# First batch's weight pieces placed in each engine's order group by group, with three raw buffers of their own and late side loads

## Chip, cores, metric

One core of one Trainium2 chip. The metric is the device time of a run in microseconds. The kernel before has a median of 818.7 us in the runs at hand at the start.

## The reference, cut to what matters

```python
# x (8, 8, 512, 64), state (8, 8, 32, 64)  -> attention both ways, concatenated: 4352 tokens x 512
# then, with w_in (512, 2048) and w_out (2048, 512):
h = x @ w_in
sp = np.maximum(h, 0.0) + np.log1p(np.exp(-np.abs(h)))   # softplus
g = h * erf(sp)
return (g @ w_out).astype(np.float32)
```

The weights arrive as float64, 16 MB in all. The kernel makes float32 of them on the chip.

## The kernel before

Batch 0 is worked in four groups of 512 hidden features. Its weights come in 16 pieces of 1 MB (two of w_in and two of w_out for each group). A piece is fetched raw, then converted by two passes of ScalarE (ACT) and three of VectorE (DVE):

```python
def weight(dst, src, shape, tag, bufs):
    ...
    raw = act.tile([P, 2 * shape[0] * i], U32, name=tag, bufs=bufs)
    nc.sync.dma_start(out=raw.rearrange("p (o i) -> p o i", i=2 * i), in_=src.bitcast(U32))
    ...
    nc.scalar.activation(out=dst, in_=hi.bitcast(F32), func=ACTF.Copy, scale=2.0 ** -112)   # L108
    nc.scalar.activation(out=lo, in_=lo, func=ACTF.Copy, scale=2.0 ** -29)                  # L109
    nc.vector.tensor_scalar(d, d, 3, None, op0=ALU.logical_shift_left)                      # L110
    nc.vector.tensor_tensor(d, d, lo, op=ALU.add)                                           # L111
    nc.vector.scalar_tensor_tensor(out=d, in0=hi, ...)                                      # L112

def weights_in(j):   weight(w_in[:, j], ..., "raw", 2)
def weights_out(g):  weight(w_out[:, t:t + 2, :], ..., "hs", 2)    # two pieces
...
def hidden(b, fts, t0, n):
    hs = act.tile([P, 4, S], F32, name="hs")          # the same two "hs" buffers as w_out's raw pieces
    s = act.tile([P, 4, S], F32, name="s")
    for i in range(4):
        hp = ps_h.tile([P, S], F32, name="h")         # two banks
        ...                                           # matmuls, L269
        nc.scalar.activation(out=s[:, i, :], in_=hp, func=ACTF.Softplus)    # L271
        nc.vector.tensor_copy(hs[:, i, :], hp)                              # L272
    nc.scalar.activation(out=s, in_=s, func=ACTF.Erf)                       # L273
    return s, hs, nc.vector.tensor_tensor(s, s, hs, op=ALU.mult)            # L274
...
for g, (first, second) in enumerate(groups):
    if b == 0 and g > 0:
        weights_in(2 * g)
        weights_in(2 * g + 1)
        mixed(0, g)                # PE mixes states into w_in: m (L253), copies by ACT and DVE (L255)
        weights_out(g)
        if g == 2:
            load_st()              # states of batches 1 to 7
    ...
    before, gT = gT, first()       # hidden(g)
    ...
    if pending is not None:
        pending()                  # project(g - 1), L279
```

The program's text is not the order in the queues: a scheduler at build time puts each engine's instructions in order by what it expects to be ready first. `tc.issue_after(x)` says that what is traced inside comes behind x on x's engine. It is an order of issue, no wait.

Of the kernel before, what the change touches and what calls it, by code (L numbers as in the profile page):

```python
# [8 lines left out]
F32 = mybir.dt.float32  # L9
U32 = mybir.dt.uint32  # L10
ALU = mybir.AluOpType
ACTF = mybir.ActivationFunctionType
# [4 lines left out]
def kernel(  # L17
# [17 lines left out]
    nc = tc.nc  # L35
    B, H, S, D = x.shape
    Ns = state.shape[2]
    d_model, d_ff = moe_w_in.shape
    P = 128
    NI = H // 2  # L40
    NC = S // P
    NK = d_model // P
    NF = d_ff // P
    GF = 4
    NG = NF // GF
# [5 lines left out]
    const = ctx.enter_context(tc.tile_pool(name="const", bufs=1))  # L51
# [5 lines left out]
    act = ctx.enter_context(tc.tile_pool(name="act", bufs=2))  # L57
# [11 lines left out]
    def load_x(b, queues=(nc.sync,)):  # L69
        t = xin.tile([P, NC, H, D], F32, name="x")  # L70
        for h in range(H):
            queues[h % len(queues)].dma_start(out=t[:, :, h, :],
                                              in_=x[b, h].rearrange("(p c) d -> p c d", c=NC))
        x_t[b] = t
# [3 lines left out]
    for e in range(2):  # L78
        nc.sync.dma_start(out=st[:, 0, D * e:D * e + D],
                          in_=state[0].rearrange("(i e) n d -> e i n d", e=2)[e])  # L80
# [9 lines left out]
    w_in = const.tile([P, NF // 2, NK, 2 * P], F32, name="w_in")  # L90
    w_out = const.tile([P, NF, d_model], F32, name="w_out")

    def weight(dst, src, shape, tag, bufs):




        if src.dtype == F32:
            nc.sync.dma_start(out=dst, in_=src)
            return  # L100
        i = shape[1]
        raw = act.tile([P, 2 * shape[0] * i], U32, name=tag, bufs=bufs)
        nc.sync.dma_start(out=raw.rearrange("p (o i) -> p o i", i=2 * i), in_=src.bitcast(U32))
        words = raw.rearrange("p (n w) -> p n w", w=2)
        lo, hi = words[:, :, 0], words[:, :, 1]
        dst = dst.rearrange("p o i -> p (o i)")
        d = dst.bitcast(U32)
# [4 lines that stand above are left out]
        nc.vector.scalar_tensor_tensor(out=d, in0=hi, scalar=0x80000000, in1=d,  # L112
                                       op0=ALU.bitwise_and, op1=ALU.bitwise_or)
# [3 lines left out]
    def weights_in(j):  # L117
        weight(w_in[:, j],
               moe_w_in[:, 2 * P * j:2 * P * j + 2 * P].rearrange("(k p) f -> p k f", p=P),
               (NK, 2 * P), "raw", 2)  # L120

    def weights_out(g):
        for t in range(GF * g, GF * g + GF, 2):
            weight(w_out[:, t:t + 2, :],
                   moe_w_out[P * t:P * t + 2 * P].rearrange("(t p) e -> p t e", p=P),
                   (2, d_model), "hs", 2)

    spare = ps_o.tile([P, d_model], F32, name="o3")

# [10 lines left out]
    def states(b):  # L140

        ps = ps_at.tile([P, P], F32, name="at")
        nc.tensor.transpose(out=ps, in_=st[:, b, :], identity=ident)
        stT[b] = keep.tile([P, P], F32, name="stT")
        nc.scalar.copy(stT[b], ps)
# [92 lines left out]
    def mixed(b, g, parts=1):  # L238

        m_t[b, g] = mix.tile([P, 2, gw], F32, name="m")  # L240
        for j in range(parts):
            ends = mixed_part(b, g, j, parts)
        return ends

    def mixed_part(b, g, j, parts):
        n = gw // parts
        mg = m_t[b, g][:, :, n * j:n * j + n]
        fs = slice(2 * g + j, 2 * g + j + 2 // parts)
        ps = [ps_at.tile([P, gw], F32, name="at")[:, 0:n] for _ in range(2)]
        for i in range(NI):  # L250
            for e in range(2):
                r, q = slice(D * e, D * e + D), slice(Ns * i, Ns * i + Ns)
                nc.tensor.matmul(out=ps[e][q, :], lhsT=stT[b][r, q],  # L253
                                 rhs=w_in[r, fs, i, :], start=True, stop=True)
        return nc.scalar.copy(mg[:, 0], ps[0]), nc.vector.tensor_copy(mg[:, 1], ps[1])  # L255

    def hidden(b, fts, t0, n):



        hs = act.tile([P, 4, S], F32, name="hs")
        s = act.tile([P, 4, S], F32, name="s")
        m = S // n
        for i in range(4):
            hp = ps_h.tile([P, S], F32, name="h")
            for j in range(m):
                ops = pairs(b, fts[m * i + j], slice(t0, t0 + n))
                for k, (lhsT, rhs) in enumerate(ops):
                    nc.tensor.matmul(out=hp[:, n * j:n * j + n], lhsT=lhsT, rhs=rhs,  # L269
                                     start=(k == 0), stop=(k == len(ops) - 1))  # L270
            nc.scalar.activation(out=s[:, i, :], in_=hp, func=ACTF.Softplus)  # L271
            nc.vector.tensor_copy(hs[:, i, :], hp)  # L272
        nc.scalar.activation(out=s, in_=s, func=ACTF.Erf)  # L273
        return s, hs, nc.vector.tensor_tensor(s, s, hs, op=ALU.mult)  # L274

    def project(gT, g, acc):
        for r in range(NC):
# [12 lines left out]
    E2 = d_model // 2  # L290
# [4 lines left out]
    T = {}  # L295

    def combine_w():
        T[1], T[2] = (act.tile([P, 2 * GF * P * 2], U32, name="raw", bufs=2).bitcast(F32)
                      .rearrange("p (g i e) -> p g i e", i=GF, e=E2) for _ in range(2))
        T[4] = const.tile([P, NG // 2, GF, E2], F32, name="T4")  # L300
        sub = lambda o, x, y: nc.vector.tensor_tensor(o, x, y, op=ALU.subtract)  # L301
        sub(T[1], B12, B11)
        sub(T[2], B22, T[1])
        sub(T[4], B21, T[2])

        def last():
            sub(B12, B22, B12)
            T[3] = B12
        return last
# [42 lines left out]
    def put_x(b, h):  # L352
        rows = out[TB * b:TB * b + S].rearrange("(p c) e -> c p e", c=NC)

        def go(r, ot):
            nc.sync.dma_start(out=rows[2 * h + r], in_=ot)
        return go
# [7 lines left out]
    def pairs(b, f, toks):  # L365
        g, fs = f // GF, slice(P * (f % GF), P * (f % GF) + P)
        if b < B:
            return [(m_t[b, g][:, e, fs], aT[b][:, e, toks]) for e in range(2)]
        return [(w_in[:, f // 2, k, P * (f % 2):P * (f % 2) + P], sT[:, k].rearrange("p b n -> p (b n)")[:, toks])
                for k in range(NK)]  # L370
# [4 lines left out]
    def plain(b):  # L375

        box = []

        def project_(g, gT):
            if g == 0:  # L380
                box.extend(tiles(NC))
            project(gT, g, box)
            if g == NG - 1:
                store(box, lambda r, ot: put_x(b, r // 2)(r % 2, ot))
        for g in range(NG):
            yield lambda g=g: hidden(b, range(GF * g, GF * g + GF), 0, S), \
                lambda gT, g=g: project_(g, gT[0])
# [26 lines left out]
    rest, on_act, on_dve = attention(0, begin)  # L414
    with tc.issue_after(on_act.ins), tc.issue_after(on_dve.ins):
        weights_in(1)
    on_act, on_dve = mixed(0, 0, 2)
    with tc.issue_after(on_act.ins), tc.issue_after(on_dve.ins):
        weights_out(0)
    pending = last = gT = None  # L420
    for b in range(B + 1):
        if b == 0:
            groups = plain(b)
        elif b < B:
            groups = fast(b, 2, lambda h, b=b: put_x(b, h))
        else:
            groups = fast(b, 1, lambda h: put_s)
        for g, (first, second) in enumerate(groups):
            if b == 0 and g > 0:
                weights_in(2 * g)  # L430
                weights_in(2 * g + 1)
                mixed(0, g)
                weights_out(g)
                if g == 2:
                    load_st()
            if b + 1 < B and g == (2 if b == 0 else 0):
                load_x(b + 1)
                states(b + 1)
            before, gT = gT, first()
            if b == 0 and g == 2:  # L440
                with tc.issue_after(before[2].ins):
                    rest()
            if pending is not None:
                pending()
            if last is not None:
                last()
                last = None
            if b == 0 and g == NG - 1:
                last = combine_w()

            def pending(gT=gT, second=second):
                second(gT)
            if b + 1 < B and (b or g > 1):
                for i in [g] if b else [2 * g - 4, 2 * g - 3]:
                    mixed(b + 1, i)
                if g == (NG - 1 if b == 0 else 1):
                    attention(b + 1)[0]()
# [31 lines left out]
```

## Time and profile before

| | before |
|---|---|
| median of the runs at the start, us | 818.7 |
| span of the profiled run, us | 815.4 |
| first hidden matmul of batch 0, us | 25.05 |
| mix of group 1 starts (second w_in piece of group 1 done), us | 44.20 |
| TensorE's longest wait from 20 to 62 us | 6.4 us, for the copy L272 |
| granted clock, 25 to 60 us | 0.82 |

A matmul in float32 leaves two records. In a row, a record of 128x512 takes 0.43 to 0.45 us at the full granted clock (eight in 3.60 us) and up to twice that at half. In a timeline row the columns are start, duration, engine, line, operation, tiles, count, and in brackets the idle time just before it with what ended it.

### The profile page before, as it was taken

Reading aid. Unit: us, or ns where it says so; the run is one execution under the profiler, and the core shown is the slowest. Engines: PE = TensorE matmul, PEld = TensorE weight load, DVE = VectorE, ACT = ScalarE, POOL = GpSimd, SP = SyncE. Lnnn points to the kernel's source line nnn. Section 1 sums busy time; section 2 is a strip of 40 time slices with the busy share of each in tenths; the row PEclk is TensorE's granted clock in tenths of the full one; section 3 lists DMA queues with packets and bytes.
Section 4 is the critical chain, followed back from the end, with each engine's and each line's share of the span. In section 5 each row is a group of like instructions: output and inputs, shape, how many; then the busy total and the mean of one; then the engine's idle time right before and its main releaser. Section 6 shows DMA issues by size and latency. Waiting matters only on the chain.

```text
span 815.4 us, 10488 instructions
## 1 busy us (share of the span) xinstructions
PE 790.0 (97%) x4460; PEld 605.4 (74%) x4460; DVE 428.6 (53%) x626; ACT 369.4 (45%) x465; POOL 0.7 (0%) x6
## 2 busy tenths in 40 slices
PE   7679999999999999999999999999999999999997
PEld 5234334678888788878887888878887888888886
DVE  3899545438454644556453844555454745443431
ACT  5688534545333833345333633373334533333220
POOL 0000000000000000000000000000000000000000
PEclk9699999999999999999999999999999999999999
DMA  9774401201100020002000110000000000000000
GB/s 276 214 258 146 112 1 39 66 0 41 39 1 26 1 79 0 27 1 79 0 27 1 29 50 1 27 1 27 1 27 1 27 1 27 1 26 1 27 1 26
DMA packets 47414, 35.27 MB, mean 43 GB/s; under 512 B 36872, under 2 KB 36872, under 8 KB 47368
## 3 DMA queue, kind: packets, MB, share of 16 engines
q1 hardware_dynamic: 45256, 34.09, 13.6%
q10 hardware_dynamic: 2112, 0.52, 0.3%
q8 instruction: 35, 0.57, 0.3%
q14 instruction: 11, 0.09, 0.0%
HBM read 25.69 MB, written 8.91 MB: 42 GB/s over the span
## 4 chain that ended last, share of the span: by engine, by line
PE 83%; ACT 3%; DVE 3%; DMA 1%; issue 1%
PE o L332 45%; PE h L269 27%; PE at L253 3%; PE o L279 3%; PE at L154 1%; PE at L177 1%; ACT L271 1%; PE at L212 1%; PE at L224 1%; PE at L195 1%; ACT s L271 1%; DVE s L274 1%; DMA hs<-in_moe_w_out_dram 1%; DVE raw L301 1%; ACT s L273 0%
## 5 line engine op out<-in xcount | busy, mean ns | idle before, releaser
L269 PE MATMUL h<-aT,m 128*128 128x256 f32 (+1 forms) x960 | 245.3, 403 | 10.6 <-DVE hs L272 7.2
L269 PEld LDWEIGHTS h<-aT,m 128*128 128x128 f32 x960 | 179.1, 192 | 76.3 <-issue 36.7
L272 DVE COPY hs<-h 128x512 f32<-128x512 f32 x136 | 93.4, 689 | 200.9 <-ACT s L271 200.9
L271 ACT ACTIVATE s<-h 128x512 f32<-128x512 f32 x136 | 80.4, 597 | 172.1 <-PE h L269 171.7
L274 DVE TENSOR_TENSOR s<-s,hs 128x2048 f32<-128x2048 f32 x34 | 77.9, 2292 | 77.1 <-ACT s L273 77.1
L332 PE MATMUL o<-raw,hs 128*128 128x256 f32 x480 | 115.7, 380 | 0.0
L332 PE MATMUL o<-w_out,s 128*128 128x256 f32 x480 | 115.0, 379 | 0.6 <-DVE s L274 0.6
L332 PE MATMUL o<-w_out,hs 128*128 128x256 f32 x480 | 113.4, 379 | 0.0
L332 PEld LDWEIGHTS o<-w_out,hs 128*128 128x128 f32 x480 | 91.2, 190 | 12.4
L332 PEld LDWEIGHTS o<-w_out,s 128*128 128x128 f32 x480 | 90.2, 190 | 13.2 <-DVE s L274 1.5
L332 PEld LDWEIGHTS o<-raw,hs 128*128 128x128 f32 x480 | 90.2, 190 | 12.3
L255 ACT COPY m<-at 128x512 f32<-128x512 f32 (+1 forms) x33 | 18.9, 571 | 158.2 <-PE at L253 158.2
L273 ACT ACTIVATE s<-s 128x2048 f32<-128x2048 f32 x34 | 65.0, 1911 | 0.4
L279 PE MATMUL o<-w_out,s 128*128 128x512 f32 x128 | 58.8, 598 | 0.0
L332 PE MATMUL o<-T,s 128*128 128x256 f32 x240 | 56.7, 379 | 0.0
L271 ACT ACT_TABLE_LOAD x40 | 51.3, 1283 | 0.7
L332 PEld LDWEIGHTS o<-T,s 128*128 128x128 f32 x240 | 45.1, 190 | 5.9
L255 DVE COPY m<-at 128x512 f32<-128x512 f32 (+1 forms) x33 | 22.2, 673 | 47.3 <-PE at L253 47.3
L279 PEld LDWEIGHTS o<-w_out,s 128*128 128x128 f32 x128 | 23.3, 190 | 30.1 <-issue 29.0
L273 ACT ACT_TABLE_LOAD x34 | 43.6, 1283 | 0.6
L253 PE MATMUL at<-w_in,stT 64*32 64x512 f32 (+1 forms) x528 | 39.6, 595 | 2.1 <-DVE w_in L112 1.3
L343 ACT COPY m<-o 128x256 f32<-128x256 f32 x15 | 5.6, 373 | 57.7 <-PE o L332 57.7
(73 smaller groups left out, 567.6 us busy)
## 6 DMA issues: line engine op xcount, KB each, us to landing
raw<-in_moe_w_in_dram SPq DMA_DIRECT2D x8, 1024.0 KB, 5.6
hs<-in_moe_w_out_dram SPq DMA_DIRECT2D x8, 1024.0 KB, 5.0
out_dram<-ot SPq DMA_DIRECT2D x32, 256.0 KB, 2.4
x<-in_x_dram SPq DMA_DIRECT2D x60, 128.0 KB, 2.9
x<-in_x_dram ACTq DMA_DIRECT2D x4, 128.0 KB, 3.6
out_dram<-ot SPq DMA_DIRECT2D x8, 64.0 KB, 1.7
st<-in_state_dram SPq DMA_DIRECT2D x8, 56.0 KB, 9.5
st<-in_state_dram SPq DMA_DIRECT2D x2, 32.0 KB
```

Source lines behind the costliest of these rows:

```text
L154: nc.tensor.transpose(out=xp[:, P * c:P * c + P], in_=xt[:, c, 2 * i:2 * i + 2, :], identity=ident)
L177: on_pe = nc.tensor.transpose(out=s1[:, NI * c:NI * c + NI, :], in_=sc[:, e, P * c:P * c + P], identity=ident)
L195: nc.tensor.transpose(out=ps[:, P * c:P * c + P], in_=a[:, e, NI * c:NI * c + NI, :], identity=ident)
L253: nc.tensor.matmul(out=ps[e][q, :], lhsT=stT[b][r, q], rhs=w_in[r, fs, i, :], start=True, stop=True)
L255: return nc.scalar.copy(mg[:, 0], ps[0]), nc.vector.tensor_copy(mg[:, 1], ps[1])
L269: nc.tensor.matmul(out=hp[:, n * j:n * j + n], lhsT=lhsT, rhs=rhs, start=(k == 0), stop=(k == len(ops) - 1))
L271: nc.scalar.activation(out=s[:, i, :], in_=hp, func=ACTF.Softplus)
L272: nc.vector.tensor_copy(hs[:, i, :], hp)
L273: nc.scalar.activation(out=s, in_=s, func=ACTF.Erf)
L274: return s, hs, nc.vector.tensor_tensor(s, s, hs, op=ALU.mult)
L279: nc.tensor.matmul(out=acc[r], lhsT=gT[:, i, P * r:P * r + P], rhs=w_out[:, GF * g + i, :], start=(g == 0 and i == 0), stop=(g == NG - 1 a ...
L332: nc.tensor.matmul(out=acc[bank][:, E2 * c:E2 * c + E2], lhsT=lhs[:, i, :], rhs=rhs[:, g, i, :], start=(first and i == 0 and c == 0), stop ...
```

## The change

Its intent: bring each weight piece to ScalarE and VectorE where it is due, so that pieces needed late (w_out) do not stand ahead of work needed at once, and give raw pieces buffers that nothing else holds. State and x(1) loads wait until the last weight piece has been issued, and batch 1 is prepared in the last group.

```diff
-        raw = act.tile([P, 2 * shape[0] * i], U32, name=tag, bufs=bufs)
+        raw = act.tile([P, 2 * shape[0] * i], U32, name="raw", bufs=3)
 ...
+        banks = []
         for i in range(4):
 ...
+            banks.append((nc.scalar.activation(... Softplus), nc.vector.tensor_copy(hs[:, i, :], hp)))
         nc.scalar.activation(out=s, in_=s, func=ACTF.Erf)
 ...
-        T[4] = const.tile([P, NG // 2, GF, E2], F32, name="T4")
+        T[1], T[2], T[4] = (act.tile(..., name="raw", bufs=3) ... for _ in range(3))
 ...
+    def weights(g, banks):
+        if g + 1 < NG:
+            for j in range(2):
+                on_act, on_dve = banks[2 * j + 1]
+                with tc.issue_after(on_act.ins), tc.issue_after(on_dve.ins):
+                    weights_in(2 * g + 2 + j)
+            on_act, on_dve = mixed(0, g + 1)
+        else:
+            on_act, on_dve = banks[3]
+        with tc.issue_after(on_act.ins), tc.issue_after(on_dve.ins):
+            weights_out(g)
 ...
-            if b == 0 and g > 0:
-                weights_in(2 * g)
-                weights_in(2 * g + 1)
-                mixed(0, g)
-                weights_out(g)
-                if g == 2:
+            if b == 0 and g == 3:
+                with tc.issue_after(fetched[-1].ins):
                     load_st()
+                    load_x(1)
+                states(1)
 ...
             before, gT = gT, first()
+            if b == 0:
+                weights(g, gT[3])
 ...
-            if b + 1 < B and (b or g > 1):
-                for i in [g] if b else [2 * g - 4, 2 * g - 3]:
+            if b + 1 < B and (b or g == 3):
+                for i in [g] if b else range(NG):
                     mixed(b + 1, i)
```

In the changed file line numbers are a little higher: conversion L111 and L112 on ACT, L113 to L115 on DVE; mix L256 and its copies L258; hidden L273, softplus L275, copy L276; Erf L277; product L278; projection L283.

More of the change, by code (lines that the diff above doesn't have):

```diff
@@ L91, with weight @@
     w_out = const.tile([P, NF, d_model], F32, name="w_out")
-    def weight(dst, src, shape, tag, bufs):
+    fetched = []
+    def weight(dst, src, shape):
         if src.dtype == F32:
-            nc.sync.dma_start(out=dst, in_=src)
+            fetched.append(nc.sync.dma_start(out=dst, in_=src))
             return
         i = shape[1]
-        raw = act.tile([P, 2 * shape[0] * i], U32, name=tag, bufs=bufs)
-        nc.sync.dma_start(out=raw.rearrange("p (o i) -> p o i", i=2 * i), in_=src.bitcast(U32))
+        raw = act.tile([P, 2 * shape[0] * i], U32, name="raw", bufs=3)
+        fetched.append(nc.sync.dma_start(out=raw.rearrange("p (o i) -> p o i", i=2 * i),
+                                         in_=src.bitcast(U32)))
         words = raw.rearrange("p (n w) -> p n w", w=2)
@@ L119, in weights_in @@
                moe_w_in[:, 2 * P * j:2 * P * j + 2 * P].rearrange("(k p) f -> p k f", p=P),
-               (NK, 2 * P), "raw", 2)
+               (NK, 2 * P))
     def weights_out(g):
@@ L125, in weights_out @@
                    moe_w_out[P * t:P * t + 2 * P].rearrange("(t p) e -> p t e", p=P),
-                   (2, d_model), "hs", 2)
+                   (2, d_model))
     spare = ps_o.tile([P, d_model], F32, name="o3")
@@ L270, in hidden @@
                                      start=(k == 0), stop=(k == len(ops) - 1))
-            nc.scalar.activation(out=s[:, i, :], in_=hp, func=ACTF.Softplus)
-            nc.vector.tensor_copy(hs[:, i, :], hp)
+            banks.append((nc.scalar.activation(out=s[:, i, :], in_=hp, func=ACTF.Softplus),
+                          nc.vector.tensor_copy(hs[:, i, :], hp)))
         nc.scalar.activation(out=s, in_=s, func=ACTF.Erf)
-        return s, hs, nc.vector.tensor_tensor(s, s, hs, op=ALU.mult)
+        return s, hs, nc.vector.tensor_tensor(s, s, hs, op=ALU.mult), banks
     def project(gT, g, acc):
@@ L297, in combine_w @@
     def combine_w():
-        T[1], T[2] = (act.tile([P, 2 * GF * P * 2], U32, name="raw", bufs=2).bitcast(F32)
-                      .rearrange("p (g i e) -> p g i e", i=GF, e=E2) for _ in range(2))
-        T[4] = const.tile([P, NG // 2, GF, E2], F32, name="T4")
+        T[1], T[2], T[4] = (act.tile([P, 2 * GF * P * 2], U32, name="raw", bufs=3).bitcast(F32)
+                            .rearrange("p (g i e) -> p g i e", i=GF, e=E2) for _ in range(3))
         sub = lambda o, x, y: nc.vector.tensor_tensor(o, x, y, op=ALU.subtract)
@@ L416 @@
         weights_in(1)
-    on_act, on_dve = mixed(0, 0, 2)
-    with tc.issue_after(on_act.ins), tc.issue_after(on_dve.ins):
-        weights_out(0)
+    mixed(0, 0, 2)
+    def weights(g, banks):
[9 more added lines that the diff above has]
+            weights_out(g)
     pending = last = gT = None
@@ L428 @@
         for g, (first, second) in enumerate(groups):
-            if b == 0 and g > 0:
-                weights_in(2 * g)
-                weights_in(2 * g + 1)
-                mixed(0, g)
-                weights_out(g)
-                if g == 2:
+            if b == 0 and g == 3:
+                with tc.issue_after(fetched[-1].ins):
                     load_st()
-            if b + 1 < B and g == (2 if b == 0 else 0):
+                    load_x(1)
+                states(1)
+            elif 0 < b < B - 1 and g == 0:
                 load_x(b + 1)
@@ L439 @@
             before, gT = gT, first()
-            if b == 0 and g == 2:
+            if b == 0:
+                weights(g, gT[3])
+            if b == 0 and g == 3:
                 with tc.issue_after(before[2].ins):
```

## The prediction

> **What bounds the kernel now.** I read the page first: the busy shares and the 40 slices.
>
> ```profile
> PE 790.0 (97%) x4460; PEld 605.4 (74%) x4460; DVE 428.6 (53%) x626; ACT 369.4 (45%) x465; POOL 0.7 (0%) x6
> ...
> PE   7679999999999999999999999999999999999997
> ...
> DVE  3899545438454644556453844555454745443431
> ACT  5688534545333833345333633373334533333220
> ...
> PEclk9699999999999999999999999999999999999999
> DMA  9774401201100020002000110000000000000000
> ```
>
> One slice is 20.4 us. TensorE (PE) is the bound almost everywhere; the exceptions are the first three slices, where PE is at 6 to 7 tenths, its clock falls to 6 tenths, and VectorE (DVE), ScalarE (ACT) and the DMA are busy together. That is the first batch, in which each of 16 weight pieces (1 MB of float64) is fetched and turned into float32 by ACT and DVE. The change touches that stage only. Where in it is PE short of work? Busy times in two stretches (PE busy, its count, granted clock, DMA share, GB/s):
>
> ```profile
> 25.00:60.30 35.30, 24.51 (x76) 0.82 0.75 231
> 60.30:149.60 89.30, 88.10 (x462) 1.00 0.25 78
> ```
>
> At 25 us the first hidden matmul starts; at 149.6 us batch 1 is running. From 60.3 us on PE is 99% busy at the full clock, so whatever the conversions do there is already hidden. Before 60.3 it is not. The waits of PE from 20 to 62 us (total, times, longest) and the timeline of PE and of DVE say why:
>
> ```profile
> PE h L269 <- DVE hs L272: 6.4, 1, 6.4
> PE h L269 <- ACT m L255: 3.1, 1, 3.1
> PE at L195 <- DVE xT L190: 2.7, 1, 2.7
> PE at L253 <- DVE w_in L112: 1.3, 1, 1.3
> ...
> 29.70 1.13 PE L269 MATMUL h<-aT,m 128*128 128x512 f32 x2
> 37.27 5.68 PE L269 MATMUL h<-aT,m 128*128 128x512 f32 x8 [6.45 <-DVE hs L272]
> 44.20 1.09 PE L253 MATMUL at<-w_in,stT 64*32 64x512 f32 x16 [1.26 <-DVE w_in L112]
> 48.38 5.26 PE L269 MATMUL h<-aT,m 128*128 128x512 f32 x8 [3.08 <-ACT m L255]
> ```
>
> ```profile
> 31.42 0.69 DVE L110 TENSOR_SCALAR w_out<-w_out 128x1024 uint32<-128x1024 uint32 x1
> 32.43 1.23 DVE L111 CUSTOM_DVE_ANT_0 w_out<-hs,w_out 128x2048 uint16<-128x2048 uint16 x1 [0.32 <-ACT hs L109]
> 33.57 0.69 DVE L110 TENSOR_SCALAR w_out<-w_out 128x1024 uint32<-128x1024 uint32 x1
> 34.17 1.22 DVE L112 SCALAR_TENSOR_TENSOR w_out<-hs,w_out 128x1024 uint32<-128x1024 uint32 x1
> 35.31 1.22 DVE L111 CUSTOM_DVE_ANT_0 w_out<-hs,w_out 128x2048 uint16<-128x2048 uint16 x1
> 36.44 0.68 DVE L272 COPY hs<-h 128x512 f32<-128x512 f32 x1
> ```
>
> The first hidden banks are computed by 29 us, but the copy that empties a bank (L272) comes at 36.44, behind the two w_out pieces of group 0, which nobody needs until the projection at 53.48. With two hidden banks, PE stops for 6.45 us. After that the clock is low: eight records in 5.68 us, 0.71 us each, against 0.45 (3.60 for eight) at 56.91.
>
> **What the Trainium skill says.** "TensorE: Matmul & The Clock Gate", section Part 1: after an idle window of about 3.4 us PE falls to half rate and needs about as long of work to return. The trace agrees: granted clock 0.50 at 36 to 40 us after the 6.45 us gap. The same page (Architectural detail) says ACT and DVE are strict FIFO, so placement in the queue decides; the wait on L272 is just that. "DMA: Bandwidth & Descriptors", section Anatomy of one DMA: a DMA's semaphore wait happens on the issuing sequencer; so a fetch that waits for a raw buffer holds back every later transfer of its queue. The trace agrees: the SyncE queue waited 22.1 us for L112 of w_in, 16.4 us for L112 of w_out, 12.4 us for the product L274 (the hs tile, shared with w_out's raw data).
>
> **The change part by part.**
> (1) Arithmetic is not changed. A piece still costs DVE 0.69 + 1.22 + 1.22 = 3.1 us (L110, L111, L112) and ACT 1.15 + 1.15 = 2.3 us. 16 pieces are 50 us of DVE and 37 us of ACT, as before.
> (2) Order. In group g of batch 0, w_in pieces of g+1 come behind hidden banks 1 and 3 on ACT and DVE, and both w_out pieces of g behind the mix of g+1. So L272 no longer waits behind w_out. A group then holds on DVE 4 x 3.1 + 4 x 0.68 (L272) + 2.29 (L274) + 0.68 (L255) = 18.1 us; on PE, 16 hidden records and 32 projection records at 0.43 plus a mix of 1.1 = 21.8 us. DVE fits under PE by about 3.7 us a group, once the projections run.
> (3) Buffers: three raw ones instead of two raw and two hs. A piece's turn-round is about 5.6 us of landing (page, DMA issues) plus some 5 us of conversion, so three give one piece per 3.5 us; a group needs four in 21.8 us. Not a limit. The first burst shrinks from 4 MB to 3 MB.
> (4) State and x(1) loads go behind the last weight fetch, out of the early queue (6 state loads took SyncE 8.40 us from 8.89 on). No compute waits for them then. The preparation of batch 1 (four mixes 4.4 us, attention 7.7 us of PE; L301 9.2 us of DVE) moves to the end of batch 0, beside projections of groups 2 and 3 (27.6 us of PE).
>
> What it gives, walked through with these durations (an estimate). Nothing before 25 us changes: softmax and two pieces keep DVE full from 12.9 us. Banks 0 and 1 run from 25 to about 28.8, the second half of the mix at 29 to 30, banks 2 and 3 from about 30.6 to 34, since their copies come in time: the 6.45 us gap goes. But w_in piece 3 only starts behind bank 3: ACT 35.2 to 37.6, DVE to about 40; so the mix of group 1 runs at 40 to 41 (before: 44.2), after an idle of about 6 us. Hence a new wait of much the same length, and a cold clock again, for hidden group 1 at about 42 (before: 48.4), ending at 50 to 52. The w_out pieces (6.2 us of DVE, with L274 and the L272 copies between them) end at about 50. So at 52 us both hidden groups are done and project 0 begins. Before, that state came at 60.34 with 8 projection records already done (8 x 0.43 = 3.4), i.e. at 56.9. Gain **about 5 us**, up to 8 to 9 if the scheduler lays conversions tightly. From there on PE is the bound in both, with the same work. I add 1 us for fewer small bubbles at the seams of 60 to 150 us: 6 us, 818.7 to **812.5**.
>
> A ceiling: from 25 to 60.3 us PE did 42 records x 0.43 = 18.1 us plus under 2 us of mixes; so at most 35.3 - 20 = 15 us can be had there. 2% are 16.4 us. A gain over 2% would need the first 25 us too, which the change hardly touches.
>
> **Rivals.**
> (a) The wait only moves: PE waits for w_in piece 3 through L112, instead of L272. Speaks for it: DVE is 88 to 99% busy from 20 to 80 us, so work is reordered on a full engine. Against: what is delayed, w_out, is not due until the projection. In full strength: 1 to 2 us gain, 817.
> (b) The late preparation of batch 1 opens a gap at 100 to 145 us: the chain st, x(1), mixes, attention took from 121.9 to 145.7 before and now starts behind the last weight fetch plus 11 us of state issues and 6 us of x issues. Against: I expect them landed at about 100, with 27.6 us of projections to cover. If it fails: 5 to 10 us lost, 816 to 822.
> (c) Fetches become the limit with three buffers: ACT, strictly in order, would stand at L108 with the softplus behind it. Against: turn-round above, and before only 6.9 us of ACT waits for fetches in all, 5.0 of them late. If so, 2 to 4 us lost per group at most, 815 to 822.
> (d) All gaps go and the clock stays up: 10 to 14 us, 805 to 809.
>
> **Range and chances.** The middle is my walk, 812.5. The low end 807.0 is (d) in part, the high end 818.0 is (a), or (b) eating the gain; outside it 2 in 10. Faster by over 2% (under 802.6): 0.03, since the ceiling of that stretch is below it. Slower by over 2%: 0.02, only if (b) and (c) come together. Within 2%: 0.95.
>
> **What would show it.** Right: L272 comes within a microsecond or so after its softplus in group 0; PE's 6.4 us wait on L272 is gone; the first projection follows a finished hidden group 1 at about 50 to 53 us; batch 1's steady pattern of 89.05 us per batch is unchanged and only begins earlier by 5 to 7 us; PE over 60 to 140 us stays at 98% or more. Rival (a) shows as PE waiting on L253 for w_in L112 by 5 us or more at about 34 to 42 us; (b) as PE idle for aT, m or stT after 95 us; (c) as ACT idle at L108 for a DMA. The prediction is wrong if the first hidden matmul moves by over 3 us from 25, if PE has gaps after 60 us, or if the scheduler places conversions elsewhere than the order of the text suggests.

## The result, and the profile after

No change: a median of 819.99 us over 4 runs against 819.16 for the kernel before in the same rounds, ratio 1.0007 (95% interval 0.9982 to 1.0031). A ratio here and below is the mean time of one kernel's fast runs over that of the other's fast runs of the same rounds, so not quite the ratio of the medians. The gain of about 6 us did not come. In five more rounds the ratio was 1.0011.

The page of the changed kernel, busy tenths in 40 slices of 20.5 us:

```profile
PE   7779999999999999999999999999999999999997
...
DVE  3577785457445554547453744555454745353431
...
PEclk9769999999999999999999999999999999999999
```

DVE is less full than before in the second and third slice (5 and 7 tenths for 8 and 9), and the clock is down in the third slice too. So the work was not crowded out by a full engine; something waits. Busy times of the two kernels from 25 to 60 us (PE, weight loads, DVE, ACT and POOL busy with counts, granted clock, DMA share, GB/s), before and then after:

```profile
25.00:60.00 35.00, 24.21 (x76) 9.67 (x73) 31.55 (x36) 29.48 (x31) 0.00 (x0) 0.82 0.75 229
```

```profile
25.00:60.00 35.00, 24.28 (x72) 9.00 (x69) 22.41 (x25) 20.28 (x23) 0.00 (x0) 0.73 0.41 140
```

TensorE got nothing out of it, while DVE and ACT are 9 us less busy each and the clock is lower. TensorE's waits from 20 to 200 us after the change, and its timeline in the critical stretch:

```profile
PE at L256 <- DVE w_in L115: 10.1, 2, 9.8
...
PE h L273 <- DVE hs L276: 0.2, 1, 0.2
```

```profile
32.48 3.67 PE L273 MATMUL h<-aT,m 128*128 128x512 f32 x8 [0.25 <-DVE hs L276]
45.91 1.96 PE L256 MATMUL at<-w_in,stT 64*32 64x512 f32 x16 [9.76 <-DVE w_in L115]
48.59 6.50 PE L273 MATMUL h<-aT,m 128*128 128x512 f32 x8 [0.71 <-ACT m L258]
```

The wait for the hidden copy is gone (6.4 us to 0.2). In its place stands one of 9.8 us for the last pass over w_in, so that the mix of group 1 starts at 45.91 us, 1.7 us later than before. But the hidden matmuls of group 1 start at the same time, 48.59 us against 48.38, because the kernel before lost 3.08 us more just ahead of them: there ACT's copy of the mix stood behind Erf. Its ACT rows:

```profile
44.65 1.28 ACT L273 ACT_TABLE_LOAD   x1
45.95 1.91 ACT L273 ACTIVATE s<-s 128x2048 f32<-128x2048 f32 x1
47.76 0.57 ACT L255 COPY m<-at 128x512 f32<-128x512 f32 x1
```

So one wait took the place of three. TensorE's waits for a tile from 25 to 62 us add up to 10.8 us before (6.45, 1.26 and 3.08) and 10.7 us after (0.25, 9.76 and 0.71), and that goes with the "no change". After the idle time the first eight hidden records of group 1 take 6.50 us, 0.81 each, against 5.26 us before and 3.60 at the full clock. What were ACT and DVE doing in the changed kernel? Their timelines in that stretch, ACT and then DVE:

```profile
36.68 1.14 ACT L111 ACTIVATE w_in<-raw 128x1024 f32<-128x1024 f32 x1
37.84 1.28 ACT L277 ACT_TABLE_LOAD   x1
39.14 1.91 ACT L277 ACTIVATE s<-s 128x2048 f32<-128x2048 f32 x1
40.95 1.13 ACT L112 ACTIVATE raw<-raw 128x1024 uint32<-128x1024 uint32 x1
```

```profile
38.46 0.68 DVE L113 TENSOR_SCALAR w_in<-w_in 128x1024 uint32<-128x1024 uint32 x1
41.08 2.29 DVE L278 TENSOR_TENSOR s<-s,hs 128x2048 f32<-128x2048 f32 x1 [1.94 <-ACT s L277]
43.29 1.22 DVE L114 CUSTOM_DVE_ANT_0 w_in<-raw,w_in 128x2048 uint16<-128x2048 uint16 x1
44.54 1.23 DVE L115 SCALAR_TENSOR_TENSOR w_in<-raw,w_in 128x1024 uint32<-128x1024 uint32 x1
```

The second w_in piece of group 1 is cut open. Between ACT's two passes over it lie a table load and the Erf of group 0; between DVE's first and second pass lie idle time and the product of group 0. The projection that needs Erf and product starts only at 54.92 us. In queues that run in the order given, as these rows do, three instructions that nobody waits for yet delay the piece that TensorE waits for. `issue_after` had said where the piece may begin at the earliest. It had not said what stays behind it.

### The profile page after: what moved, and what is told of

The parts are those of the page before. It is cut to its first block, busy times and chain, and to the rows that moved or that the text cites. A ratio compares the mean times of both kernels' runs of the same rounds, so it can differ in the third digit from the quotient of the medians.

```text
span 819.1 us, 10493 instructions
## 1 busy us (share of the span) xinstructions
PE 791.8 (97%) x4460; PEld 605.8 (74%) x4460; DVE 429.0 (52%) x626; ACT 369.4 (45%) x465; POOL 0.7 (0%) x6
## 4 chain that ended last, share of the span: by engine, by line
PE 89%; ACT 5%; DVE 3%; issue 2%; DMA 1%; SPq 0%; DVEq 0%
PE o L335 44%; PE h L273 30%; PE at L256 4%; PE o L283 4%; PE at L157 1%; PE at L198 1%; PE at L180 1%; PE at L227 1%; PE at L215 1%; ACT s L277 1%; ACT L275 1%; ACT L277 1%; DMA x<-in_x_dram 1%; DVE w_in L114 1%; ACT s L275 1%
## 5 line engine op out<-in xcount | busy, mean ns | idle before, releaser
L273 PE MATMUL h<-aT,m 128*128 128x256 f32 (+1 forms) x960 | 245.4, 403 | 1.0 <-ACT m L258 0.7
L273 PEld LDWEIGHTS h<-aT,m 128*128 128x128 f32 x960 | 179.1, 192 | 66.6 <-issue 35.6
L276 DVE COPY hs<-h 128x512 f32<-128x512 f32 x136 | 93.4, 689 | 187.6 <-ACT s L275 187.6
L275 ACT ACTIVATE s<-h 128x512 f32<-128x512 f32 x136 | 80.4, 597 | 166.9 <-PE h L273 166.6
L278 DVE TENSOR_TENSOR s<-s,hs 128x2048 f32<-128x2048 f32 x34 | 77.9, 2292 | 80.1 <-ACT s L277 80.1
L258 ACT COPY m<-at 128x512 f32<-128x512 f32 (+1 forms) x33 | 18.9, 573 | 163.4 <-PE at L256 163.4
L277 ACT ACTIVATE s<-s 128x2048 f32<-128x2048 f32 x34 | 64.9, 1910 | 0.4
L283 PE MATMUL o<-w_out,s 128*128 128x512 f32 x128 | 59.2, 602 | 1.3 <-DVE w_out L115 1.3
L335 PE MATMUL o<-raw,s 128*128 128x256 f32 x240 | 56.7, 379 | 0.0
L275 ACT ACT_TABLE_LOAD x40 | 51.3, 1283 | 0.7
L258 DVE COPY m<-at 128x512 f32<-128x512 f32 (+1 forms) x33 | 22.2, 674 | 54.9 <-PE at L256 54.9
L256 PE MATMUL at<-w_in,stT 64*32 64x512 f32 (+1 forms) x528 | 40.1, 609 | 10.6 <-DVE w_in L115 10.1
L335 PEld LDWEIGHTS o<-raw,s 128*128 128x128 f32 x240 | 45.2, 190 | 5.9
L283 PEld LDWEIGHTS o<-w_out,s 128*128 128x128 f32 x128 | 23.0, 190 | 32.3 <-issue 29.7
L277 ACT ACT_TABLE_LOAD x34 | 43.6, 1283 | 0.6
```

The source lines that it names most:

```text
L256: nc.tensor.matmul(out=ps[e][q, :], lhsT=stT[b][r, q], rhs=w_in[r, fs, i, :], start=True, stop=True)
L258: return nc.scalar.copy(mg[:, 0], ps[0]), nc.vector.tensor_copy(mg[:, 1], ps[1])
L273: nc.tensor.matmul(out=hp[:, n * j:n * j + n], lhsT=lhsT, rhs=rhs, start=(k == 0), stop=(k == len(ops) - 1))
L275: banks.append((nc.scalar.activation(out=s[:, i, :], in_=hp, func=ACTF.Softplus), nc.vector.tensor_copy(hs[:, i, :], hp)))
L276: nc.vector.tensor_copy(hs[:, i, :], hp)))
L283: nc.tensor.matmul(out=acc[r], lhsT=gT[:, i, P * r:P * r + P], rhs=w_out[:, GF * g + i, :], start=(g == 0 and i == 0), stop=(g == NG - 1 a ...
```

## The experiments

The theory (**A**): the wait was moved. The start of group 1 is set by when its second w_in piece is done, and the scheduler's order put Erf and the product inside that piece. Rivals: **B**, the gain came and was lost again in the late preparation of batch 1; **C**, ACT and DVE are full, so no order helps; **E**, the shared hs buffers were the whole loss before, and the placed order spoiled the gain; **F**, a part of the loss is the half clock. The capital letters belong to the experiments; A is the prediction's rival (a), B its (b). The recorded texts name runs by short labels: e1 is the Erf variant, e15 the same in group 0 alone, e3 "both", e12 "first piece at once", e11 the longer warm-up, e13 e12 with it, and e4 and e6 are the runs on buffers and on late preparation. The kernels were run on two chips, each with its own runs of the kernel before, and all gave correct results. Differences in us between two kernels are differences of medians.

### The changed kernel again

> The changed kernel once more, so that the variants are compared with it on the same chip. Every theory: 0.998 to 1.003 of the kernel before (the first four runs gave 1.0007), with TensorE waiting about 9.8 us for the second w_in piece of group 1 (L115) at 36 to 46 us.

Measured: 820.12 us, ratio 1.0011 (0.9996 to 1.0027); the wait for L115 was again 9.8 us.

### Erf and product behind the second piece (A against B and C)

The edit, cut; the comments are added here:

```diff
-        nc.scalar.activation(out=s, in_=s, func=ACTF.Erf)
-        return s, hs, nc.vector.tensor_tensor(s, s, hs, op=ALU.mult), banks
+        ends = fetch(banks) if fetch is not None else ()   # traces the two w_in pieces of the next group,
+        with ExitStack() as order:                          # gives the last pass on ACT and on DVE
+            for end in ends:
+                order.enter_context(tc.issue_after(end.ins))
+            nc.scalar.activation(out=s, in_=s, func=ACTF.Erf)
+            on_dve = nc.vector.tensor_tensor(s, s, hs, op=ALU.mult)
+        return s, hs, on_dve, banks
 ...
```

> The changed kernel with Erf and the product of each group of batch 0 queued behind the conversion of the second w_in piece; nothing else differs. Theory A (the wait moved: the L276 wait is gone, and the wait for the second w_in piece took its place because Erf with its table load, 1.28 + 1.91 us, and the product, 2.29 us, sit inside that conversion): the 9.8 us wait falls to 5 to 6 us, and the time by 3 to 5 us against the changed kernel, to 0.995 to 0.997 of before. Rival B (the loss is in the late preparation of batch 1): the wait falls, but the gaps after 90 us grow by the same, time within 1 us of the changed kernel. Rival C (ScalarE and VectorE are full, order cannot matter): time within 1 us, wait unchanged or moved again.

Measured: **813.19 us**, ratio 0.9926 (0.9908 to 0.9943), 6.9 us under the changed kernel. ACT's timeline and TensorE's of this kernel:

```profile
36.73 1.25 ACT L111 ACTIVATE w_in<-raw 128x1024 f32<-128x1024 f32 x1
37.76 1.24 ACT L112 ACTIVATE raw<-raw 128x1024 uint32<-128x1024 uint32 x1
39.01 1.28 ACT L281 ACT_TABLE_LOAD   x1
40.31 1.91 ACT L281 ACTIVATE s<-s 128x2048 f32<-128x2048 f32 x1
```

```profile
41.95 1.96 PE L256 MATMUL at<-w_in,stT 64*32 64x512 f32 x16 [5.75 <-DVE w_in L115]
44.63 5.12 PE L273 MATMUL h<-aT,m 128*128 128x512 f32 x8 [0.71 <-ACT m L258]
```

The same instructions in another order: the wait falls by 4.0 us, from 9.76 to 5.75. The eight hidden records behind it take 5.12 instead of 6.50 us in these two profiles, but that difference is not shown to come from the shorter wait: they took 6.20 us in the other profile of the changed kernel, and 6.17 in the next run, whose wait is as short as here. A is shown, and the gain is more than my 3 to 5 us. B and C are refuted as the main cause: the engines had room.

### The same in group 0 alone

```diff
+                                     (lambda banks: pieces(g, banks)) if g + 1 < NG else None, g == 0)
 # hidden(..., fetch, hold): only where hold is true do Erf and the product come behind the pieces
```

> e1 with Erf and the product held behind the second w_in piece in group 0 alone; groups 1 and 2 keep the order of the changed kernel. Theory A, as the traces of e1 and the changed kernel have it (of 6.9 us, 4.0 are the shorter wait in group 0, 1.4 the clock that returns sooner, the rest, about 1.5, small waits for w_out and at seams in groups 1 and 2): 4.5 to 6 us under the changed kernel, 0.994 to 0.996 of before. Against it: the same as e1 (0.9926), then group 0 is the whole; or under 3 us, then groups 1 and 2 hold more than their waits show.

Measured: 815.03 us, ratio 0.9954 (0.9938 to 0.9970), as expected: 0.57% under the changed kernel's 1.0011 (4.7 us), of 0.85% for all groups. So about two thirds lie in group 0. The expectation counted 1.4 us for a clock that returns sooner; this run's own profile does not bear that out (6.17 us for the eight records). In groups 1 and 2 the split piece costs less: from 62 to 210 us TensorE waits 1.3 us for w_out here and in the changed kernel, and not at all in the Erf variant. TensorE has a projection to do meanwhile (in the changed kernel from 60.93 to 70.54 us without a break); that this is the reason was not tested.

### Side loads and preparation of batch 1 as before (B)

```diff
-            if b == 0 and g == 3:
-                with tc.issue_after(fetched[-1].ins):
-                    load_st()
-                    load_x(1)
+            if b == 0 and g == 2:
+                load_st()
+                load_x(1)
 ...
-            if b + 1 < B and (b or g == 3):
-                for i in [g] if b else range(NG):
+            if b + 1 < B and (b or g > 1):
+                for i in [g] if b else [2 * g - 4, 2 * g - 3]:
```

> The changed kernel with the state and x(1) loads and the mixes of batch 1 where the kernel before has them (from group 2 on, not queued behind the last weight fetch). Theory A: the 9.8 us wait stays, time within 1.5 us of the changed kernel. Rival B: 2 to 4 us less than the changed kernel (0.995 to 0.998 of before), found after 90 us. Rival C says nothing different from A.

Measured: 819.88 us, ratio 1.0008 (0.9990 to 1.0026), 0.2 us from the changed kernel. The wait is still 9.8 us. B has nothing to show here. A second test, on the variant "both" below, where TensorE waits less:

> e3 with the state and x(1) loads and batch 1's mixes as the kernel before has them. e6 showed no difference while TensorE waited for w_in; with that wait shorter, rival B gets a second test. Theory A: within 1.5 us of e3 (0.990 to 0.9935 of before). Rival B: 2 us or more under e3 (0.989 or less).

Measured: 813.79 us, ratio 0.9934 (0.9919 to 0.9948). That is no gain over "both" (0.9917); if anything, the late preparation is better by about 1 us, and the two intervals overlap.

### Three raw buffers alone, on the kernel before (E)

```diff
-        raw = act.tile([P, 2 * shape[0] * i], U32, name=tag, bufs=bufs)
+        raw = act.tile([P, 2 * shape[0] * i], U32, name="raw", bufs=3)
 # and T4 in the raw pool, as in the change; nothing placed
```

> The kernel before with the three raw buffers alone (w_out no longer lands in the hs buffers, T4 in the raw pool); no placed order, side loads as before. In its queue the first hs copy now stands ahead of the w_out pieces of group 0 (nothing else holds it any more), but both w_in pieces of group 1 stand behind them. Theory A (what counts is when the second w_in piece of group 1 is done, wherever the time before it goes): the 6.4 us wait on the copy shrinks to 2 to 4 us, a wait for w_in of 4 us or more follows, time 0.998 to 1.006 of before. Rival E (the shared hs buffers were the whole loss of the kernel before, and the placed order spoiled the gain): 0.990 to 0.995 of before.

Measured: 819.17 us, ratio 0.9999 (0.9984 to 1.0015), as A has it and not E. TensorE's waits from 20 to 210 us of this kernel:

```profile
PE at L253 <- DVE w_in L112: 5.1, 1, 5.1
PE h L269 <- DVE hs L272: 4.5, 3, 4.1
```

With buffers of its own the first hs copy did move ahead of the w_out pieces (it ran at 31.12 us, with both w_out pieces behind it), which the kernel before could not do while both hs buffers held raw w_out. But the second copy stood behind most of them, and w_in came last: the mix of group 1 started at 46.83 us. (ACT also stood 3.3 us for the fetch of the last w_in piece, but DVE, which ends the piece, idled only 0.26 us for it.) TensorE's waits from 25 to 62 us add up to 10.6 us. Three kernels, three orders, one time: the mix of group 1 starts at 44.2, 45.9 and 46.8 us, the waits are 10.8, 10.7 and 10.6 us (6.9 in the Erf variant), and the whole takes 818.7 to 820.1 us. So the sum of the waits goes with the time here, and the start of the mix alone does not.

### Both pieces earlier as well ("both")

```diff
-            on_act, on_dve = banks[2 * j + 1]
+            on_act, on_dve = banks[j]            # on top of the Erf variant
```

> As e1, and the two w_in pieces also queued behind hidden banks 0 and 1 instead of 1 and 3. Theory A: the second piece is then ready by about 39 to 40 us, the wait for L115 is 2 to 5 us, the time 4 to 7 us under the changed kernel (0.992 to 0.996 of before); a small new wait on L276 (up to 1 us) may come back. Rival B: within 1 us of the changed kernel. Rival C: the gain of e1 is lost again to a wait on L276 of 3 us or more.

Measured: 812.55 us, ratio 0.9917 (0.9901 to 0.9933), only 0.6 us under the Erf variant, with overlapping intervals. The wait was 5.5 us, above the 2 to 5 us expected. The edge set the earliest place only: ACT finished the softplus of bank 0 at 30.28 us, and the scheduler still put bank 1's ahead of the first piece, which began at 31.82.

### First piece at once

DVE is idle for 4.4 us up to 31.3 us in the changed kernel, waiting for the mix. The raw piece could be worked on then (in this variant ACT took it early and waited for no fetch from 20 to 60 us).

```diff
-        weights_in(1)
+        landed = weights_in(1)
 ...
-            on_act, on_dve = banks[j]
+            on_act, on_dve = landed if g == 0 and j == 0 else banks[0 if g == 0 else j]
```

> e3 with, in group 0 only, the first w_in piece of group 1 right behind the conversion of the last piece of group 0 (VectorE and ScalarE idle 4 to 5 us there in the changed kernel) and the second behind hidden bank 0. Theory A: the wait for the second w_in piece falls from 5.5 us to 0 to 3 us and the time by 2 to 4 us against e3, to 0.986 to 0.990 of before. Rival C (engines full): the hidden banks are delayed by as much, no gain against e3.

Measured: 810.73 us, ratio 0.9890 (0.9871 to 0.9909), 0.27% under "both" in ratio, about 2.2 us. It was run at another time. The longest of TensorE's waits from 20 to 210 us that are left in group 0's start:

```profile
PE h L273 <- ACT m L258: 2.4, 1, 2.4
...
PE h L273 <- DVE hs L276: 1.4, 1, 1.4
PE at L256 <- DVE w_in L115: 0.9, 1, 0.9
```

The wait for w_in is down to 0.9 us, but part of the gain is paid back: 2.4 us for a copy of the mix, which now stands behind Erf, and 1.4 us for a hidden copy behind the first piece.

### The clock (F)

```diff
-            warm(20)
+            warm(32)          # dummy matmuls, to fill TensorE's idle 2.7 us at 18 to 20.7 us
```

> The changed kernel with 32 instead of 20 dummy matmuls ahead of the first attention's transposes, to fill TensorE's idle 2.7 us at 18 to 20.7 us; nothing else moves. Theory F (the clock is half for 21 to 30 us because of that idle time, and the phase in which the throttle falls makes the scatter of times): records of the first hidden banks go from 0.9 to 0.43 us, 2 to 3 us off the start of group 0; but the wait for the second w_in piece is set by ScalarE and VectorE behind bank 3, which moves with the banks, so the time falls by 2 to 3 us, to 0.998 of before. Against F: the clock falls all the same, or the dummies delay the transposes: 0 to +1 us.

Measured: 816.78 us, ratio 0.9972 (0.9956 to 0.9987); 0.39% in ratio, 3.2 us, under the changed kernel. The dummies and the first hidden records in this kernel:

```profile
14.22 7.31 PE L136 MATMUL o<-ident 128*128 128x128 f32 x64
...
24.73 2.84 PE L273 MATMUL h<-aT,m 128*128 128x512 f32 x6
```

In the changed kernel those six records took 5.39 us. The granted clock is 1.00 through 20 to 25 us here; there it is 0.50 from 22 to 30 us. The wait for w_in is 9.8 us in both: it starts earlier and is just as long, as F and A have it together. F is a real cost, but hardly the one that ate the gain, since the kernel before is cold there too (granted clock 0.65 from 22 to 30 us). The longer warm-up was not run on the kernel before, so how much that kernel would gain by it is open.

### Both causes reduced

> e12 with the 32 dummy matmuls of e11. If both theories A and F hold and add up: 2 to 3 us under e12, 0.983 to 0.987 of before. If the conversions of the two pieces bound the start instead of the banks, under 1 us.

Edit: "first piece at once" with `warm(32)`. Measured: **807.72 us** over 4 runs, ratio 0.9858 (0.9839 to 0.9878), 3.0 us under "first piece at once". This is the best kernel of the study, 1.4% under the kernel before and, by median, some 12 us under the changed one (of another call). It is still "same" by the mark of 2%.

### One step too far

TensorE still waits 2.4 us for ScalarE's copy of the mix behind Erf. So Erf and the product were put behind the mix's copies too:

```diff
-                ends = weights_in(2 * g + 2 + j)
-        return ends
+                weights_in(2 * g + 2 + j)
+        copied[g] = mixed(0, g + 1)
+        return copied[g]
```

> e13 with Erf and the product also behind the copies of the next group's mix. In e13 TensorE waits 2.4 us for ScalarE's copy of the mix, which stands behind Erf. Theory A: that wait falls under 0.8 us, 1.5 to 3 us under e13, 0.982 to 0.985 of before. Against it: Erf and the product come so late that the first projection, or the two w_out pieces, make a wait of 1.5 us or more: no gain.

Measured: 815.23 us, ratio 0.9954 (0.9939 to 0.9970), 7.5 us worse than the kernel it was made from. It was run at another time. TensorE's waits in it:

```profile
PE o L288 <- DVE w_out L115: 6.7, 1, 6.7
...
PE h L273 <- ACT m L258: 0.7, 1, 0.7
```

The wait aimed at went from 2.4 to 0.7 us. But the scheduler, given one more constraint, put one projection matmul ahead of the last two hidden banks, and on DVE both w_out pieces, side by side, ahead of the next hidden copies (47.93 us): 6.7 us for w_out. The same pattern as in the change itself: the wait moved.

## Why the prediction was wrong

**What bounds the kernel before, and the ceiling**: right in the main. The loss lies before 60 us, and what was moved there decided. One reading was incomplete. I put the 6.45 us wait on L272 down to queue order alone; by the code both hs buffers were full of raw w_out then, and with buffers of its own the copy did move ahead. Buffers alone gained nothing, though (0.9999). A second row was shown and not followed up: the 3.08 us wait for ACT's copy of the mix, which stood behind Erf and its table load. The instructions that later landed inside the piece were already in the way there. Two slips in the sums, on which nothing hangs: the timeline has 40 records before 60.3 us, not 42, which makes the ceiling about 16 us, and 2% under 818.7 is 802.3, not 802.6.

**The step that failed** is this one of the walk: "But w_in piece 3 only starts behind bank 3: ACT 35.2 to 37.6, DVE to about 40; so the mix of group 1 runs at 40 to 41 (before: 44.2), after an idle of about 6 us." I assumed that a piece, once begun, runs through. Measured: ACT 36.68 to 42.08 us, DVE to 45.77, the mix at 45.91, the idle time 9.76 us. The term missing from the sum is what stands inside the piece: 1.28 + 1.91 us on ACT and 2.29 us on DVE, together worth 4.0 us of wait (ACT's second pass, 1.13 us, ran beside the product). With Erf and product behind the piece the idle time was 5.75 us, as in the walk, and the mix started at 41.95 us; it started at 40.29 us in the profile of group 0 alone, where the first six records took 4.13 us, as before, and not 5.44. So the rest of this step was right within the scatter of the clock. That the Erf variant's 813.19 us lies so near my 812.5 is partly luck: some 2 of its 6.9 us come from groups 1 and 2, where the walk counted 1 us for all seams. Group 0 alone gives 0.46% under the kernel before, 3.8 us against the walk's 5.

**Rival (a)**, that the wait only moves, was named in the prediction with its mark: TensorE waiting on L253 for L112 by 5 us or more. It is what happened, at 9.8 us. I gave its full strength as a gain of 1 to 2 us; the gain was nothing, since the one wait of 9.76 us cost as much as the three that it replaced (10.7 us of waits against 10.8). Whether the longer idle time also costs more clock than before is not shown: the first eight records of group 1 took 6.50 and 6.20 us in the two profiles after, 5.26 before, but 5.36 behind the same 9.8 us in the run with the longer warm-up.

**The range** failed with it: its high end, 818.0, took rival (a) as leaving a small gain. **The chances** (0.95 for within 2%) held.

**Rival (b)**, the late preparation: refuted by two runs. **Rival (c)**, fetches: the trace after shows no wait of ACT for a fetch from 25 to 120 us; the kernel before had 6.9 us. **Rival (d)** did not come.

**First hidden matmul** unchanged: 25.19 against 25.05 us. **Where the page on the clock was used**: half rate after the gap, as it says. I used it to explain the kernel before, and left the clock out of the sum for the first banks, which take 5.39 us for six records in the profiled run after, 4.12 before. That scatters with nothing changed: the same six records of the same order took 4.78 us in the other profiled run of the changed kernel.

What stays open: why the profile of the changed kernel is 3.7 us longer than that of the kernel before (819.1 and 815.4) while the timed runs differ by 0.1%. The runs of before scatter over 4 us, and its profiled run, 817.2, lies in the low part. That the phase in which the clock falls makes this scatter was only argued. With the longer warm-up the changed kernel's six times lay within 0.6 us.

## What to carry to other kernels

When work is placed behind a mark in an in-order queue, say also what must stay behind it: a piece that TensorE waits for is only as early as its last pass, and most of what the scheduler slips between its passes is added to the wait (here 4.0 of 5.5 us). Before a reordering is built, list for the stage each instruction that could stand inside the piece on each engine and add its time to the walk; afterwards, add up the waits of the stage, and do not look only at which wait has gone. And where an idle stretch cannot be removed, keep the clock up through it: here 12 more dummy matmuls gained about 3 us, in two kernels.

## What the Trainium skill lacked or had wrong

- "TensorE: Matmul & The Clock Gate", Part 1, speaks of an idle window of about 3.4 us before the clock falls, and its table for kernels of gaps over about 3 us. Here a gap of 2.7 us was enough in all ten profiles with 20 dummies: the granted clock fell to 0.50 between 2.0 and 5.0 us after the last dummy matmul. In three of them it fell after 2.0 to 2.2 us, before the next matmul began (in the changed kernel at 20.1 us; the transposes start at 20.70). In the three profiles where dummies filled the gap it stayed at 1.00 there.
- "ScalarE: Activation LUTs", section What ACT_TABLE_LOAD costs, gives 1283 ns and another 1380 ns of drain, 2.66 us for a switch. The 1283 ns are seen. The drain is not seen here: ACT's first pass over the piece began at 36.68 and took 1.14 us, the load began at 37.84, and Erf at 39.14, so the switch took 1.32 us in all.
- "FP8 and Floating Point Precision", TensorE Precision Notes, gives float32 four passes through the array. In these traces a 128x512 matmul takes 0.86 us at the full clock and stands as two records of 0.43 us (20 dummy matmuls leave 40 records, 32 leave 64). No page that I read mentions the two records, and whether each is two passes no run here tests.
